# A copy moved to VectorE, fewer dummy matmuls, keys and conversion steps in another order, in the start of a delta-rule attention with a feed-forward block

## The chip, the cores and the metric

The kernel runs on one NeuronCore of a Trainium2 chip. The metric is the device time of one execution in microseconds, the median of several runs. Lower is better.

## The reference

The first half is a delta-rule recurrence over 768 positions for 4 batches of 8 heads of dimension 48. Its output, heads side by side, is the input of a feed-forward block of 384 to 2048 to 384 with the gate h * sigmoid(1.702 h).

```python
k_n = k / (np.linalg.norm(k, axis=-1, keepdims=True) + 1e-06)
for t in range(S):                       # S = 768, per batch and head, state is 48 x 48
    y[t]  = q[t] @ state
    v_old = state.T @ k_n[t]
    state = state + beta[t] * outer(k_n[t], v[t] - v_old)
x = y.transpose(0, 2, 1, 3).reshape(B * S, H * D)   # 3072 x 384
h = x @ w_in                                        # 384 x 2048
out = (h / (1 + exp(-1.702 * h))) @ w_out           # 2048 x 384
```

The two weights arrive in 64-bit floating point; the kernel fetches them raw, as pairs of 32-bit words, and makes 32-bit floats of them itself.

## The kernel before

**Tiling.** The 768 positions are cut into six chunks of 128, and a *unit* is one chunk of one batch with all eight heads: 24 units, numbered chunk by chunk (units 0 to 3 are chunk 0, units 4 to 7 chunk 1, and so on). In a unit the recurrence becomes: normalize the keys, make the Gram matrix `G` of the keys, solve a triangular system for `U` in four blocks of 32 positions, and form the outputs from `U`, the masked scores `M` and the state `ST`. Two units side by side give 256 tokens of feed-forward.

**Keys.** `normalize_mixed(n)` squares the keys of unit n on ScalarE (tile `ksq`), sums on VectorE (`ssq`), takes the root on GpSimd (`rn`), and adds, inverts and multiplies on VectorE. `prepare(n)` transposes them on PE (`psT`, copied to `kT`), makes `G` through `psG`, and for chunk 1 sends the 32-wide diagonal blocks of `G` to DRAM (`Nd`, four DMAs on the sync queue) and back in another layout into the tile `NT` (one DMA that waits for those four). The key buffers are `KN`, seven in turn; unit 7 uses `KN[0]` and unit 8 `KN[1]`.

**Inversion.** `invert(c)` inverts the 32 x 32 diagonal blocks of a whole chunk on VectorE, 128 blocks at once in the 128 partitions: 15 row steps on both 16 x 16 halves together, then a *join*: a transposed copy `X1` of the second half's inverse into a corner of `NT`, four products `P<-NT,YB` with sums into `NT`, and four products `P<-NT` with sums into `YB`. The result goes into tiles `XB`, one per unit. For chunk 0 it goes there by a transpose on VectorE, for later chunks through DRAM. Chunk 0's join copy is on ScalarE, chunk 1's on VectorE, those of later chunks on ScalarE.

**Solve.** One *hop* is a call of `together`: for some units a block solve (`psU<-V,XB`, copied to `US` or `U` on ScalarE), for others the effect of the block on the rows below (`psR<-US,G`, subtracted from `V` on VectorE). Chunk 0 is done as two pairs of units in eight hops each, with `put_out` behind each pair (`psY`, `ST`, `last`, `xT`; for the second unit of a pair six small DMAs `xT<-last` on the sync queue). Between the hops stand three kinds of other work, each handed out in fixed numbers:

- `fill(n)` advances the conversion of the weights by n steps. A piece of a weight takes five steps, on VectorE with one pass on ScalarE; the pieces of w_in are named ("in", i, e) and those of w_out ("out", f). At the end of some pieces the next raw pieces are fetched.
- `ahead_of(preparing, n)` advances the keys of chunk 1 (`keys()`) by n steps. A table of start times, `(0, 3, 6, 14, 17)`, says at which step units 4 to 8 begin.
- `warm(n)` puts n dummy matmuls on PE (`ps_warm<-ident`), which keep PE active. `NY` of them wait for a memset on VectorE and stand in chunk 0's join; `NW` stand at the start, `NU` and `NA` in the hops.

`feed()` advances the first feed-forward group of the chunk-0 tokens (`ph<-xT,w_in`, then the gate into `gT`) by half a group.

**Order.** The calls in this start are pinned (`tc.keep_in_program_order`), so each engine and each DMA queue executes them in the order in which the Python code makes them; an instruction whose operand is missing holds those behind it on its engine or queue. Behind the second pair comes a loop that converts what is left of w_in, then `invert(1)` with `feed()` in between, then the rest of `hidden`. From there on `woven(n)` runs for n = 3 to 24: it weaves the hops of neighbouring units, the keys of unit m = n + 5 and the feed-forward from `queue`. In its first steps `both_written` is in that queue, which multiplies with w_out piece by piece as the pieces are converted (`po<-w_out,gT`). The keys of units 9 and later are loaded in `follow(n)` on GpSimd's queue.

Of the kernel before, what the change touches and what calls it, by code (L numbers as in the profile page):

```python
# [18 lines left out]
def kernel(  # L19
# [32 lines left out]
    HB = 2  # L52
# [2 lines left out]
    GB = 8  # L55

    XR = DP - D
    NW, NA, NY, NU = 14, 3, 60, 11
    NQ = DFF // 4
    NPC = DFF // 8  # L60
    NS = C * C + C
# [232 lines left out]
    def fill(n):  # L294
        for _ in range(n):
            next(converting, None)
# [144 lines left out]
    def invert(c, b0=0, nb=B):  # L441

        np = nb * NB * H
        part = slice(b0 * NB * H, b0 * NB * H + np)
        N, Y = NT[part], YB[part]
        bc = bI[part, c].broadcast_to([np, BS, BS])
        tt, red = vec.tensor_tensor, vec.tensor_reduce
        if c > 0:
            tt(N, N, bc, op=ALU.mult)
            yield 0.0  # L450
        HS = BS // 2

        def dots(o, a, b, ny, nx, nk, negate):

            P = wk.tile([128, ny, nx, nk], F32, tag="P", name="P")[part]
            tt(P, a, b, op=ALU.mult)
            red(o, P, axis=AX.X, op=ALU.add, negate=negate)

        def halves(t):

            return [t[:, s * HS : (s + 1) * HS, s * HS : (s + 1) * HS] for s in range(2)]


        Yf = Y.rearrange("p j i -> p (j i)")
        Nf = N.rearrange("p i k -> p (i k)")
        step = HS * BS + HS

        def diag(t, off, dims):
            return bass.AP(t.tensor, t.offset + off, [t.ap[0], [step, 2]] + dims)

        for i in range(1, HS):
            P = wk.tile([128, 2, i, i], F32, tag="P", name="P")[part]
            tt(
                P, diag(Nf, i * BS, [[0, i], [1, i]]), diag(Yf, 0, [[BS, i], [1, i]]),
                op=ALU.mult,
            )
            red(diag(Yf, i, [[BS, i]]), P, axis=AX.X, op=ALU.add, negate=True)
            yield 0.0


        X1 = N[:, 0:HS, HS:]
        if c == 1:
            vec.tensor_copy(X1, halves(Y)[1].rearrange("p l i -> p i l"))
        else:
            act.activation(X1, halves(Y)[1].rearrange("p l i -> p i l"), ACT.Copy)
        A = N[:, 0:HS, 0:HS]
        N10, Y0 = N[:, HS:, 0:HS], halves(Y)[0]
        Q = 4
        for j in range(0, HS, Q):
            n = HS - j  # L490
            dots(
                A[:, j : j + Q, :],
                N10[:, :, j:].rearrange("p (o l) k -> p o l k", o=1).broadcast_to([np, Q, HS, n]),
                Y0[:, j : j + Q, j:].rearrange("p j (o k) -> p j o k", o=1).broadcast_to([np, Q, HS, n]),
                Q, HS, n, False,
            )
            yield 0.0
        for i in range(0, HS, Q):
            n = i + Q
            if c == 0 and i == HS - 2 * Q:  # L500
                warm(NY, vec.memset)
            dots(
                Y[:, 0:HS, HS + i : HS + i + Q],
                A[:, :, 0:n].rearrange("p j (o l) -> p j o l", o=1).broadcast_to([np, HS, Q, n]),
                X1[:, i : i + Q, 0:n].rearrange("p (o i) l -> p o i l", o=1).broadcast_to([np, HS, Q, n]),
                HS, Q, n, True,
            )
            yield 0.0
        if c == 0:
            T = wk.tile([128, BS, BS], F32, tag="P", name="YT")  # L510
            vec.transpose(T.rearrange("p d i -> p i d"), Y.rearrange("p j i -> p i j"))
            for b in range(B):
                XB = wk.tile([128, H, BS], F32, tag="XB", name="XB", bufs=4)
                tt(
                    XB, T[:, b * H : (b + 1) * H],
                    zs[:, 5, b].broadcast_to([128, H, BS]), op=ALU.mult,
                )
                inverse[b] = XB
                yield 0.0
            return  # L520
        YS = wk.tile([128, BS, BS], F32, tag="P", name="YS")[part]
        tt(YS, Y, bc, op=ALU.mult)
        dma = sync if c < 3 else nc.sync.dma_start
        groups = [range(b0, b0 + nb)]
        back = {}
        for bs in groups:
            for b in bs:
                back[b] = dram.tile([H * C, BS], F32, tag="Yd", name="Yd", bufs=4)
                dma(
                    out=back[b].rearrange("(p j) i -> p j i", j=BS),  # L530
                    in_=YS[(b - b0) * NB * H : (b - b0 + 1) * NB * H],
                )
            for b in bs:
                XB = wk.tile([128, H, BS], F32, tag="XB", name="XB", bufs=4)
                dma(out=XB, in_=back[b].rearrange("(h t) i -> t h i", h=H))
                inverse[c * B + b] = XB
        yield 0.0
# [233 lines left out]
    def run(work):  # L771
        for _ in work:
            pass
# [38 lines left out]
    def follow(n):  # L812

        dma = sync if n <= B else nc.sync.dma_start
        if n + B < len(units):
            load(n + B, ((QP, q),), dma)
        m = n - 1 + len(KN)
        if m < len(units):
            load(m, ((KN, k),), nc.gpsimd.dma_start)
        if n - 1 + B < len(units):  # L820
            load_values(n - 1 + B, dma)
        if n % HB == 0 and n > B:
            h = (n - 1) // HB
            gT = []
            queue.append(hidden(xTs[h], gT, slice(0, NTH), 1.3))
            queue.append(written(*units[h * HB], gT))
            xTs.pop(h)
# [12 lines left out]
    def woven(n, share):  # L840

        nonlocal inverting
        A, B_, D_ = steps.pop(n - 1, None), steps.get(n), steps.get(n + 1) or NoStep()
        m = n + B + 1
        K = (normalize if n > 6 else normalize_mixed)(m) if m < len(units) else iter(())
        P = prepare(m) if m < len(units) else iter(())
        if m in begun:  # L850
            K, P = iter(()), begun.pop(m)
        if n % HB == 1 and B < n and n + 1 + HB < len(units):
            inverting = invert(*units[n + 1 + HB], HB)
        ahead = STEPS[:3] if n % HB == 1 else STEPS[3:]

        next(K, None)
        together([(B_, 1)], [(A, 2)])
        run(D_.scored)
        next(K, None)
        ahead_of(inverting, ahead[0])  # L860
        spend(share / 3)

        together([(A, 3), (D_, 0)], [(B_, 1)])
        next(K, None)
        ahead_of(inverting, ahead[1])
        spend(share / 6)
        next(P, None)
        spend(share / 6)

        together([(B_, 2)], [(D_, 0)])  # L870
        if A:
            A.queries()
            A.outputs(True)
        run(P)
        ahead_of(inverting, ahead[2])
        if n % HB == 0:
            run(inverting)
        spend(share / 6)
        next(new_step(n + 2).scored, None)
        spend(share / 6)  # L880
        follow(n)
# [80 lines left out]
    def keys():  # L962

        def unit(n):
            yield from normalize_mixed(n)
            yield from prepare(n)

        begun[2 * B] = prepare(2 * B)

        def first(n):  # L970
            yield from normalize_mixed(n)
            next(begun[n])

        work = [unit(n) for n in range(B, 2 * B)] + [first(2 * B)]
        for t in range(26):
            for u, begin in enumerate((0, 3, 6, 14, 17)):
                s = t - begin
                if s >= 0 and s % 2 == 0:
                    next(work[u], None)
            yield  # L980
        for w in work:
            run(w)
# [21 lines left out]
    def feed(n=1):  # L1004
        for _ in range(n):
            while ffn and next(ffn[0], None) is None:
                ffn.pop(0)
# [8 lines left out]
    path = hops(*pair[2:])  # L1016
    for i in range(2 * NB):
        together(*next(path))
        fill(2)
        if i > 2:  # L1020
            feed()
        warm(NU if i < 3 else 4)
        ahead_of(preparing, 2)
        if 3 <= i < 6:
            fetch_out(i - 3)
    for s in pair[2:]:
        put_out(s)
        feed()
        fill(2)
    ffn.append(hidden(xTs[1], gTs[1], slice(0, NTH), 1.3, True))  # L1030
    xTs.pop(0), xTs.pop(1)
    load(B + 2, ((QP, q),), sync)
    while not ("in", 3, 1) in done:
        fill(2)
        feed()
        ahead_of(preparing, 1)
    run(preparing)
    first = new_step(B)
    run(first.scored)
    inverting = invert(1)  # L1040
    for i in range(25):
# [41 lines left out]
```

## Time and profile before

| | |
|---|---|
| median of the runs | 792.83 us (3 runs, 791.43 to 795.32) |
| the profiled execution | 792.6 us, span of its profile 790.9 us |
| mean granted TensorE clock | 0.965 |
| PE busy | 754.1 us (95% of the span) |
| PE weight load busy | 564.5 us (71%) |
| VectorE (DVE) busy | 456.5 us (58%) |
| ScalarE (ACT) busy | 243.0 us (31%) |
| GpSimd (POOL) busy | 127.1 us (16%) |
| dummy matmuls `ps_warm` | 199, 29.9 us |

Times are microseconds from the start of the span. PE is the matmul side of TensorE, PEld its weight load, SPq the sync engine's DMA queue. A line of a timeline gives start, length, engine, source line, operation, output<-input, sizes and count, and in brackets how long the engine was idle ahead of it and what ended that. A line of the waits gives who waited for whom, the time in total, the number of times and the longest. The slices are 40 equal parts of the span, 19.8 us each, with the busy share in tenths. A list of instructions shows a float matmul twice, since it is made in two passes. Nearly all source lines are the helper's line 102, so rows are told apart by their tiles.

### The profile page before, as it was taken

How to read it: one execution, taken by the hardware profiler on the slowest of the kernel's cores; microseconds unless marked ns; L12 is line 12 of the kernel's file. 1: busy time of each engine (PE TensorE's matmuls, PEld its weight loads, DVE VectorE, ACT ScalarE, POOL GpSimd, SP SyncE). 2: the span in 40 equal slices, each digit the busy share in tenths (PEclk: the TensorE clock that was granted, in tenths of full speed). 3: DMA queues.
4: the chain of work that ended last, by engine and by line, in shares of the span. 5: the costliest groups of instructions: out<-in, count | busy, mean ns of one | idle time of the engine just before them, and what ended most of it. 6: DMA issues, size and time to landing. Idle time of an engine off the chain costs nothing.

```text
span 790.9 us, 18899 instructions
## 1 busy us (share of the span) xinstructions
PE 754.1 (95%) x8199; PEld 564.5 (71%) x8199; DVE 456.5 (58%) x934; ACT 243.0 (31%) x537; POOL 127.1 (16%) x132
## 2 busy tenths in 40 slices
PE   7788999598899999999999999999999999999997
PEld 6677888355568768768678678678678678677684
DVE  6778778996895666766666766756756531100000
ACT  4555552244233323223223223223223123121110
POOL 6301410001121212212212211221210000000000
PEclk8589999799999999999999999999999999999999
DMA  9941940453323231231222232241230020000000
GB/s 164 176 58 39 256 96 8 111 162 72 75 64 70 55 86 42 58 90 35 64 74 52 56 95 43 46 103 42 46 76 12 21 43 2 12 15 1 25 1 20
DMA packets 130657, 50.72 MB, mean 64 GB/s; under 512 B 105408, under 2 KB 126016, under 8 KB 130576
## 3 DMA queue, kind: packets, MB, share of 16 engines
q1 hardware_dynamic: 128112, 41.08, 24.1%
q0 software_dynamic: 2464, 8.46, 4.4%
q8 instruction: 64, 1.05, 0.6%
q14 instruction: 17, 0.14, 0.1%
HBM read 32.08 MB, written 16.25 MB: 61 GB/s over the span
## 4 chain that ended last, share of the span: by engine, by line
PE 81%; DVE 12%; DMA 3%; ACT 2%; issue 2%; SPq 1%; POOL 0%; DVEq 0%; POOLq 0%; ACTq 0%
PE po L102 28%; PE ph L102 26%; PE psY L102 5%; PE psU L102 5%; PE psQ L102 4%; PE psG L102 4%; PE ps_warm L102 3%; PE psT L102 3%; DVE P L102 3%; DVE YB L102 2%; DVE w_out L102 2%; PE psR L102 2%; DVE tmp L102 2%; DMA Nd<-G 1%; DVE NT L102 1%
## 5 line engine op out<-in xcount | busy, mean ns | idle before, releaser
L102 PE MATMUL po<-w_out,gT 128*128 128x384 f32 x768 | 269.5, 500 | 11.7 <-ACT w_out L102 8.9
L102 PE MATMUL ph<-xT,w_in 128*128 128x256 f32 x1152 | 261.5, 383 | 0.3
L102 PEld LDWEIGHTS ph<-xT,w_in 128*128 128x128 f32 x1152 | 214.7, 190 | 32.7 <-issue 1.5
L102 PEld LDWEIGHTS po<-w_out,gT 128*128 128x128 f32 x768 | 143.1, 193 | 103.9 <-ACT w_out L102 9.3
L102 DVE TENSOR_TENSOR V<-V,psR 64x384 f32<-64x384 f32 (+1 forms) x96 | 53.4, 556 | 198.0 <-PE psR L102 192.7
L102 ACT ACTIVATE gT<-ph 128x512 f32<-128x512 f32 x96 | 56.5, 596 | 140.1 <-PE ph L102 140.0
L102 DVE TENSOR_TENSOR P<-NT,YB 64x8 f32<-64x8 f32 (+31 forms) x190 | 89.2, 469 | 5.3
L102 ACT COPY US<-psU 32x384 f32<-32x384 f32 x92 | 43.2, 469 | 146.1 <-PE psR L102 128.6
L102 DVE TENSOR_REDUCE YB<-P 64x4 f32<-64x8 f32 (+31 forms) x190 | 80.9, 426 | 6.5
L102 PEld LDWEIGHTS psU<-V,XB 32*32 32x32 f32 x1536 | 57.9, 106 | 35.4 <-issue 29.0
L102 PE MATMUL psU<-V,XB 32*32 32x48 f32 x1536 | 68.6, 204 | 1.5 <-DVE YB L102 1.2
L605 POOL TENSOR_SCALAR_AFFINE_SELECT M<-M 128x1024 f32<-128x1024 f32 x20 | 24.9, 1247 | 265.9 <-DVE M L102 169.4
L102 PE MATMUL psR<-US,G 32*32 32x48 f32 x2208 | 60.4, 204 | 0.0
L102 PEld LDWEIGHTS psR<-US,G 32*32 32x32 f32 x2208 | 51.1, 106 | 1.1 <-ACT G L102 0.5
L102 PE MATMUL psQ<-QS,kT 48*128 48x176 f32 (+1 forms) x384 | 37.6, 341 | 3.7 <-ACT QS L102 3.7
L102 DVE TENSOR_TENSOR P<-NT 64x256 f32<-64x256 f32 (+7 forms) x40 | 34.0, 851 | 4.8 <-ACT NT L102 4.6
L102 PEld LDWEIGHTS psQ<-QS,kT 48*128 48x128 f32 x384 | 31.1, 209 | 6.8 <-ACT QS L102 5.6
L102 PE MATMUL ps_warm<-ident 128*128 128x256 bf16 x199 | 29.9, 309 | 5.4 <-DVE ps_warm L102 4.0
L102 PE MATMUL psG<-kT 48*128 48x128 f32 x384 | 32.3, 306 | 2.6 <-ACT kT L102 1.3
L102 DVE TENSOR_REDUCE NT<-P 64x64 f32<-64x1024 f32 (+7 forms) x40 | 32.6, 815 | 1.4
L87 POOL DMA_DIRECT2D KN<-in_k_dram x15 | 14.3, 951 | 111.5 <-PE psY L102 102.6
L102 PEld LDWEIGHTS psG<-kT 48*128 48x128 f32 x384 | 27.3, 205 | 6.0 <-ACT G L102 2.1
(98 smaller groups left out, 604.2 us busy)
## 6 DMA issues: line engine op xcount, KB each, us to landing
Nd<-G SPq DMA_DIRECT2D x16, 512.0 KB, 3.5
QP<-in_q_dram SPq DMA_DIRECT2D x24, 192.0 KB, 3.8
V<-in_v_dram SPq DMA_DIRECT2D x24, 192.0 KB, 3.3
out_dram<-o SPq DMA_DIRECT2D x24, 192.0 KB, 1.9
KN<-in_k_dram POOLq DMA_DIRECT2D x15, 192.0 KB, 3.7
NT<-Nd SPq DMA_DIRECT2D x20, 128.0 KB, 2.5
Yd<-YS SPq DMA_DIRECT2D x20, 128.0 KB, 2.4
XB<-Yd SPq DMA_DIRECT2D x20, 128.0 KB, 3.3
```

The source lines that it names most:

```text
L87: dma(out=dst[n % len(dst)][:, :, 0:D], in_=src[b, :, c * C : (c + 1) * C, :].rearrange("h p d -> p h d"),)
L102: return lambda *a, **kw: tc.keep_in_program_order(op(*a, **kw))
L605: (pool if self.n < B else nc.gpsimd).affine_select(out=self.M, in_=self.M, compare_op=ALU.is_gt, fill=0.0, base=0, pattern=[[0, H], [1, 1 ...
```

## The change

It changes the order and the number of instructions in the first 200 us; the arithmetic is the same.

- Chunk 0's join copy goes from ScalarE to VectorE (`c <= 1`).
- `NY` is 46 in place of 60, and the memset that releases these dummies stands behind the first of the join's second four products instead of the second.
- In the second pair's hops the dummies are put only in the first three hops; the four dummies in each of the other five are gone.
- The second pair's hops advance the conversion by 3 steps in place of 2 from the sixth hop on, and so does each of its two `put_out`.
- Units 7 and 8 begin their keys at steps 10 and 13 in place of 14 and 17.
- The keys of units 9 and 10 are loaded on the sync queue behind the second pair, and not on GpSimd's; they are normalized one `woven` step sooner (in n = 3 and n = 4).
- Unit 4's first step (its scores) is begun ahead of the loop that converts the rest of w_in and finished in its second turn, and not behind it.

```diff
@@ -55,7 +55,7 @@
     GB = 8
 
     XR = DP - D
-    NW, NA, NY, NU = 14, 3, 60, 11
+    NW, NA, NY, NU = 14, 3, 46, 11
     NQ = DFF // 4
     NPC = DFF // 8
     NS = C * C + C
@@ -479,7 +479,7 @@
 
 
         X1 = N[:, 0:HS, HS:]
-        if c == 1:
+        if c <= 1:
             vec.tensor_copy(X1, halves(Y)[1].rearrange("p l i -> p i l"))
         else:
             act.activation(X1, halves(Y)[1].rearrange("p l i -> p i l"), ACT.Copy)
@@ -497,7 +497,7 @@
             yield 0.0
         for i in range(0, HS, Q):
             n = i + Q
-            if c == 0 and i == HS - 2 * Q:
+            if c == 0 and i == HS - 3 * Q:
                 warm(NY, vec.memset)
             dots(
                 Y[:, 0:HS, HS + i : HS + i + Q],
@@ -815,7 +815,7 @@
         if n + B < len(units):
             load(n + B, ((QP, q),), dma)
         m = n - 1 + len(KN)
-        if m < len(units):
+        if 2 * B + HB < m < len(units):
             load(m, ((KN, k),), nc.gpsimd.dma_start)
         if n - 1 + B < len(units):
             load_values(n - 1 + B, dma)
@@ -845,10 +845,13 @@
         nonlocal inverting
         A, B_, D_ = steps.pop(n - 1, None), steps.get(n), steps.get(n + 1) or NoStep()
         m = n + B + 1
-        K = (normalize if n > 6 else normalize_mixed)(m) if m < len(units) else iter(())
+        if n < B + HB:
+            K = normalize_mixed(m + 1) if n <= B else iter(())
+        else:
+            K = (normalize if n > 6 else normalize_mixed)(m) if m < len(units) else iter(())
         P = prepare(m) if m < len(units) else iter(())
         if m in begun:
-            K, P = iter(()), begun.pop(m)
+            P = begun.pop(m)
         if n % HB == 1 and B < n and n + 1 + HB < len(units):
             inverting = invert(*units[n + 1 + HB], HB)
         ahead = STEPS[:3] if n % HB == 1 else STEPS[3:]
@@ -972,8 +975,8 @@
             next(begun[n])
 
         work = [unit(n) for n in range(B, 2 * B)] + [first(2 * B)]
-        for t in range(26):
-            for u, begin in enumerate((0, 3, 6, 14, 17)):
+        for t in range(22):
+            for u, begin in enumerate((0, 3, 6, 10, 13)):
                 s = t - begin
                 if s >= 0 and s % 2 == 0:
                     next(work[u], None)
@@ -1016,26 +1019,34 @@
     path = hops(*pair[2:])
     for i in range(2 * NB):
         together(*next(path))
-        fill(2)
+        fill(2 if i < 5 else 3)
         if i > 2:
             feed()
-        warm(NU if i < 3 else 4)
+        else:
+            warm(NU)
         ahead_of(preparing, 2)
         if 3 <= i < 6:
             fetch_out(i - 3)
     for s in pair[2:]:
         put_out(s)
         feed()
-        fill(2)
+        fill(3)
     ffn.append(hidden(xTs[1], gTs[1], slice(0, NTH), 1.3, True))
     xTs.pop(0), xTs.pop(1)
     load(B + 2, ((QP, q),), sync)
+    for n in range(2 * B + 1, 2 * B + 1 + HB):
+        load(n, ((KN, k),), sync)
+    first = new_step(B)
+    next(first.scored)
+    t = 0
     while not ("in", 3, 1) in done:
         fill(2)
         feed()
+        if t == 1:
+            run(first.scored)
         ahead_of(preparing, 1)
+        t += 1
     run(preparing)
-    first = new_step(B)
     run(first.scored)
     inverting = invert(1)
     for i in range(25):
```

## The prediction

> **What bounds the kernel now.** I read the page's slices first, then the waits, the timeline engine by engine, and the chain of waits.
>
> ```profile
> PE   7788999598899999999999999999999999999997
> DVE  6778778996895666766666766756756531100000
> PEclk8589999799999999999999999999999999999999
> ```
>
> A slice is 19.8 us. From slice 9 on PE is full, so the end moves only by what the first 200 us release: PE idle, dummies, or a late start of whatever holds PE there. From 121 to 187 us the timeline of VectorE has no pause over 0.1 us: it inverts chunk 1 (121.43 to 148.1) and converts w_out to 187.1. PE ran out of `ph` at 143.0 and waited for the first converted piece of w_out. So the start of that inversion, at 121.43, sets the end. The waits up to 200 us:
>
> ```profile
> PE po L102 <- ACT w_out L102: 8.9, 1, 8.9
> DVE P L102 <- ACT NT L102: 4.6, 1, 4.6
> PE psT L102 <- DVE KN L102: 2.3, 1, 2.3
> ```
>
> First: that gap of PE. Second: VectorE waits for chunk 0's join copy, which stands on ScalarE behind the scores' copies. Third: unit 9's transpose waits for its normalized keys; unit 10's waits 2.38 us more at 204.31. Timelines (start, length) of the first join:
>
> ```profile
> 38.35 0.66 ACT L102 ACTIVATE NT<-YB 128x256 f32<-128x256 f32 x1
> 39.04 0.86 DVE L102 TENSOR_TENSOR P<-NT 128x256 f32<-128x256 f32 x1 [4.55 <-ACT NT L102]
> 41.80 9.33 PE L102 MATMUL ps_warm<-ident 128*128 128x256 bf16 x60 [4.01 <-DVE ps_warm L102]
> ```
>
> The sync queue's, which explains 121.43 (the inversion's multiply shows "3.05 <-issue"):
>
> ```profile
> 82.35 1.01 SPq L102 DMA_DIRECT2D KN<-in_k_dram  x2
> 94.77 3.28 SPq L102 DMA_DIRECT2D Nd<-G  x4
> ...
> 109.50 0.31 SPq L102 DMA_DIRECT2D NT<-Nd  x1
> 109.86 3.68 SPq L102 DMA_DIRECT2D xT<-last  x6
> 113.58 0.58 SPq L102 DMA_DIRECT2D QP<-in_q_dram  x1
> 114.27 2.00 SPq L102 DMA_DIRECT2D Nd<-G  x4
> 119.26 0.32 SPq L102 DMA_DIRECT2D NT<-Nd  x1
> ```
>
> Unit 7's pair `Nd`, `NT` comes last, behind six `xT` pieces. And ScalarE in the second pair's third hop and later:
>
> ```profile
> 79.30 0.47 ACT L102 COPY US<-psU 32x384 f32<-32x384 f32 x1 [0.77 <-PE psR L102]
> 82.73 1.08 ACT L102 ACTIVATE G<-psG 128x512 f32<-128x512 f32 x2 [2.96 <-PE psG L102]
> 83.84 0.47 ACT L102 COPY U<-psU 32x384 f32<-32x384 f32 x1
> ...
> 90.70 0.53 ACT L102 ACTIVATE ksq<-KN 128x384 f32<-128x384 f32 x1
> ```
>
> **What the Trainium skill says.** "TensorE: Matmul & The Clock Gate", Part 1: PE starts at half clock, about 3.4 us of activity release it, an idle window takes it back. The trace agrees: granted clock 0.50 from 40.4 to 47.2, 1.00 from 47.2 to 51.0, and 0.60 from 77.2 to 81.5 after PE pauses of 1.35 and 0.68 us. The same page, "Architectural detail": ScalarE and VectorE are strict FIFO; the join copy at 38.35, right behind the `M` copies, agrees. "SBUF — State Buffer", "SBUF: two separate sides": VectorE with two SBUF inputs and GpSimd block each other; the same 256-element product took 0.86 us beside a GpSimd select at 38.53 and 0.42 at 33.62. "DMA: Bandwidth & Descriptors", "Anatomy of one DMA": a DMA's wait is made on the issuing sequencer, so it holds what is queued behind; each `NT` above issues 3 us after its `Nd` and holds the rest.
>
> **The change part by part**, against the profiled execution: 792.6 us, span 790.9 and 1.7 around it; the median of the runs is 792.83.
>
> 1. *Join copy on VectorE.* It goes behind the last row step (end 27.52). It costs 0.4 (chunk 1's took 0.39 at 133.61); the four products to 34.49 then end at 34.9. The second half took 39.04 to 46.0; one more GpSimd select now lies over it (+0.44): end 42.3. Transpose 1.96, first `XB` 0.36: inverse of unit 0 at 44.7, before at 48.4. ScalarE loses 0.55 us ahead of the scaling of V (7.3 us, end 45.7, needed for the first hop's copy only).
> 2. *46 dummies for 60, one product earlier.* PE is free at 37.8. At 0.213 us cold and 0.109 warm (from 60 in 9.33 us with the clock rising at 47.2), 46 end between 44.1 (clock up at 40.4) and 45.8 (at 43.8). So the first solve starts at 44.8 to 45.9 instead of 51.05: **gain s = 5.6** (5.15 to 6.25). The first pair's hops (2.11 us each, PE full, VectorE half idle) and its outputs keep their order and move by s.
> 3. *Keys of units 7 and 8 four steps sooner.* Unit 7's square now stands on ScalarE right behind the `US` copy (79.30), ahead of the `G` and `U` copies, and needs the key load issued at 82.35, behind six `xT` and twelve w_in pieces. Moved by s: issue 76.75; landing took 5.5 us, other loads of keys 3.7 to 7.0; I take 5.0, since GpSimd's load of w_out now comes after it: 81.75. ScalarE is free at 74.2, so it **waits about 7.5 us**. Behind it are two `G` copies (1.09), `U` (0.47) and, through `U`, the next hop's psR, VectorE's V and all that follows: `U` ends at 81.75+0.53+1.09+0.47 = 83.85, against 84.3-5.6 = 78.7 without the wait: 5.1 lost on the hops. PE then pauses some 4 us; one window at half clock costs 0 to 1.7, I take 1.2.
> 4. *No dummies from the fourth hop, three steps a fill from the sixth.* 20 dummies of 0.11 are 2.2 us less of PE, but unit 7's and 8's transposes and unit 7's Gram product (0.44+0.44+1.09) come into the hops from behind. Hops five to eight on PE: 3.4, 2.7, 3.8, 2.3 us, outputs with one `ph` group 4.45. End: 83.85+16.65+1.2 = 101.7 (before 102.8). Five conversion steps (0.7 each) move in beside this; VectorE needs 13.9 us from 82.7, ready at 96.6, so they cost nothing here; without that cover they would cost 3.5.
> 5. *VectorE behind the pair.* Sum of its rows after the second ST: 11.2 us (twelve conversion steps, four V of unit 4). Inversion ready at 101.9+11.2 = **113.1**. Unit 4's scores come sooner; PE delivers psQ from 106.8, VectorE reaches V at 107.5: nothing.
> 6. *Sync queue.* Unit 7's `Nd`, `NT` now precede `xT` and QP. First `Nd` 94.77-5.6 = 89.2; four pairs as before without 4.3 us: last `NT` lands at 121.43-5.6-4.3 = 111.5, with the measured 3.4 us of the third pair 110.3. Gram products are there in time. So VectorE is last, not the queue, and the inversion starts at 113.1: **gain 8.3**. `xT` of the second pair lands near 115; its first `ph` is due at 117.
> 7. *Keys of units 9 and 10.* Loads go from GpSimd's queue to the sync queue behind QP: two issues of 0.4 near 114, with the queue idle from 119.6 to 148.1 before; due after 135. Unit 9's 1.48 us (0.55+0.16+0.20+0.57) now fall among the w_out steps, VectorE full: -1.48; one step went ahead of the inversion: +0.36. Unit 9's psT no longer waits, but w_out's piece at 185.2 holds PE instead: 0. Unit 10's stall, where PE is full, goes: +2.38. Next there are unit 11's keys; VectorE has 0.32, 0.89 and 0.76 us of waits for PE before them and 0.93 less work, so it keeps up.
>
> Sum: 8.3+0.36-1.48+2.38 = 9.6 us; 792.6-9.6 = **783.0**.
>
> **Rivals.**
> A. *The keys land early enough or the stall is covered.* For: its load's wait on its eighth predecessor may be shorter with GpSimd's loads later. Against: seventeen sync issues, 11 us, stand before it. Then the queue bounds: start 110.3, gain 11.1+1.26 = 12.4: 780.2. Chance 0.20.
> B. *The loads of w_out and raw, pushed later by the wait, run into the Nd/NT pairs.* 2.3 MB at the 327 GB/s seen from 88 to 95 us is 7 us; if pairs take 7 instead of 5, the last `NT` is at 118 and the gain 3.4+1.26 = 4.7, or with half of s lost about 2: 788 to 791. Against: DMA was as full before. Chance 0.17.
> C. *Slower: ScalarE's wait for unit 7's keys.* Each us of later landing moves the hops and the inversion by one. From 81.75, the gain of 9.6 is used up at 91.4, that is 14.6 us after issue. For: V loads in the same stretch took 10.2; against: keys took 5.5 there. At 96 it gives 797. Chance 0.08.
> Mine: 0.55.
>
> **Numbers.** The range takes s (1.1), landing (3.7 to 7), clock (1.7), A whole and most of B: 778 to 788.5. Half a percent, 4 us, is about what a measurement of this kernel can tell from no change: limits 788.9 and 796.8. Faster 0.81 (mine, A, a third of B), same 0.14 (the rest of B, a part of C), slower 0.05.
>
> **What would show it.** Right: no wait of VectorE at the first join; first psU at 45 to 46; ScalarE idle before unit 7's square on the key load by 6 to 9 us with PE idle behind it; `NT<-NT,bI` at 113 directly behind a conversion step; no psT wait of unit 10. Wrong: no such wait on ScalarE (A); the multiply waiting for `NT` beyond 116 (B); the square after 90 (C); or PE waiting longer for w_out after 150 than 1.5 us a time.

## Result and the profile after

The changed kernel takes 783.05 us (median of 4 runs, 782.55 to 783.69), the kernel before beside it 792.55 us: ratio 0.9875, interval 0.9849 to 0.9902. In a later comparison it took 782.26 us against 789.63: 0.9897 (0.9870 to 0.9924). The kernel before spreads more (787 to 795 us), and with more runs its median was 789.6 to 789.9 in three comparisons; so the gain is rather 7 us (7.4 in the later comparison) than the 9.5 of the first four runs. The predicted 783.0 holds, and so does the predicted gain of 9.6 beside those first runs; beside the later ones it is 2 us too large. Some of its terms do not hold, and that their errors cancel is luck; this is the main matter of what follows. Three of the single runs behind the medians below took over 1.5% longer than the fastest of their kernel; the ratios leave them out, the medians do not.

The profiled execution took 782.8 us, span 780.8. Its page, the slices of 19.5 us:

```profile
PE   7898799699999999999999999999999999999997
DVE  5989679987977566666666666666665531000000
PEclk8599899879999999999999999999999999999999
```

Behind the slice with PE's gap (the 6) every slice of PE but the last shows 9. Before, two slices behind the gap showed 8, those with the key stalls of units 9 and 10. VectorE's last digits end one slice sooner. The waits up to 200 us (who waited for whom, total, times, longest):

```profile
ACT ksq L102 <- DMA KN<-in_k_dram: 7.2, 1, 7.2
PE po L102 <- ACT ksq L102: 5.2, 1, 5.2
PE psT L102 <- ACT G L102: 4.6, 3, 3.3
```

VectorE's wait for the join copy and PE's waits for normalized keys are gone. ScalarE's wait for a key load is new, and PE waits behind it. PE's gap before w_out shrank from 8.9 to 5.2 us. The timeline of the first join (start, length):

```profile
27.67 0.77 DVE L102 COPY NT<-YB 128x256 f32<-128x256 f32 x1
...
42.17 1.99 DVE L102 STREAM_TRANSPOSE YT<-YB 128x1024 f32<-128x1024 f32 x1
...
37.71 6.67 PE L102 MATMUL ps_warm<-ident 128*128 128x256 bf16 x46
44.73 0.83 PE L102 MATMUL psU<-V,XB 32*32 32x48 f32 x16 [0.35 <-issue]
```

The first solve starts at 44.73 instead of 51.05, 6.32 us sooner. Before, the dummies held it: they ended at 51.13, while the inverse of unit 0 was there at 48.4. Now the dummies end at 44.38 and the inverse comes at 44.6. Then the sync queue, ScalarE and PE in the second pair's third hop:

```profile
75.00 1.80 SPq L102 DMA_DIRECT2D KN<-in_k_dram  x2
...
80.70 0.52 ACT L102 ACTIVATE ksq<-KN 128x384 f32<-128x384 f32 x1 [7.24 <-DMA KN<-in_k_dram]
81.25 1.09 ACT L102 ACTIVATE G<-psG 128x512 f32<-128x512 f32 x2
82.36 0.47 ACT L102 COPY U<-psU 32x384 f32<-32x384 f32 x1
...
81.90 1.12 PE L102 MATMUL psT<-ident,KN 128*128 128x128 f32 x4 [3.28 <-ACT G L102]
```

The `G` and `U` copies stand behind the waiting square, as the prediction had it. The end of the second pair, the start of chunk 1's inversion (its first multiply, `NT<-NT,bI`) and the sync queue:

```profile
103.23 0.36 DVE L102 TENSOR_TENSOR ST<-psY,ST 128x192 f32<-128x192 f32 x1 [0.95 <-PE psY L102]
...
114.68 0.35 DVE L102 TENSOR_SCALAR tmp<-raw 128x384 int32<-128x384 int32 x1
114.95 1.22 DVE L102 TENSOR_TENSOR NT<-NT,bI 128x1024 f32<-128x1024 f32 x1
...
107.06 0.31 SPq L102 DMA_DIRECT2D NT<-Nd  x1
107.42 3.69 SPq L102 DMA_DIRECT2D xT<-last  x6
```

No bracket behind 114.95: the inversion comes straight behind a conversion step, 11.72 us after the last `ST`. The last `NT` was issued at 107.06, ahead of the `xT` pieces, so the queue no longer holds it. And the transposes of units 9 and 10 on PE:

```profile
178.13 0.60 PE L102 MATMUL psT<-ident,KN 128*128 128x128 f32 x4
...
196.42 0.60 PE L102 MATMUL psT<-ident,KN 128*128 128x128 f32 x4
```

Neither waits; before, each waited 2.35 to 2.38 us.

Where the 10.1 us between the two spans (790.9 and 780.8) came from, cut at the start of the inversion and at its last product, `YS<-YB,bI`, before and after:

```profile
146.85 1.23 DVE L102 TENSOR_TENSOR YS<-YB,bI 128x1024 f32<-128x1024 f32 x1
...
141.11 1.22 DVE L102 TENSOR_TENSOR YS<-YB,bI 128x1024 f32<-128x1024 f32 x1
```

Start 121.43 to 114.95, 6.48 gained; the inversion itself 25.42 to 26.16, 0.74 lost; from `YS` to the end 644.05 to 639.7, 4.35 gained. The prediction had 8.3, nothing, and 0.36 - 1.48 + 2.38 = 1.26.

### The profile page after: what moved, and what is told of

Read it like the earlier page. It is cut to its first block, busy times and chain, and to the rows that moved or that the text cites. A ratio compares the mean times of both kernels' runs of the same rounds, so it can differ in the third digit from the quotient of the medians.

```text
span 780.8 us, 18832 instructions
## 1 busy us (share of the span) xinstructions
PE 753.3 (96%) x8165; PEld 564.1 (72%) x8165; DVE 457.1 (59%) x935; ACT 243.1 (31%) x536; POOL 125.3 (16%) x130
## 4 chain that ended last, share of the span: by engine, by line
PE 83%; DVE 11%; DMA 3%; ACT 2%; issue 1%; SPq 0%; POOL 0%; DVEq 0%; POOLq 0%; ACTq 0%
PE po L102 29%; PE ph L102 27%; PE psU L102 5%; PE psY L102 5%; PE psQ L102 4%; PE psG L102 4%; PE psT L102 3%; DVE P L102 3%; PE ps_warm L102 2%; PE psR L102 2%; DVE YB L102 2%; DVE tmp L102 2%; DVE w_out L102 1%; DVE NT L102 1%; DMA KN<-in_k_dram 1%
## 5 line engine op out<-in xcount | busy, mean ns | idle before, releaser
L102 ACT ACTIVATE gT<-ph 128x512 f32<-128x512 f32 x96 | 56.5, 596 | 140.1 <-PE ph L102 140.0
L102 ACT COPY o<-po 128x384 f32<-128x384 f32 x24 | 11.5, 479 | 61.7 <-issue 39.2
L102 ACT COPY M<-psQ 128x256 f32<-128x256 f32 x68 | 22.9, 377 | 22.2 <-DVE V L102 16.1
```

What stands on the lines that cost most here:

```text
L102: return lambda *a, **kw: tc.keep_in_program_order(op(*a, **kw))
```

## The experiments

The kernels of one comparison ran on one chip beside the kernel before. Executions of one kernel spread over 1 to 13 us. The changed kernel's two medians, 783.05 and 782.26, agree, and 782.7 is the base to which the other medians are held; single effects are read from the profiles. In every diff of this section "+" is what the experiment has.

### Four parts taken back, one at a time

Base: the changed kernel, which itself did not run in this comparison. The kernel before took 789.64 us in it (787.42 to 794.02).

**Keys of units 9 and 10 as before.**

```diff
-        if 2 * B + HB < m < len(units):
+        if m < len(units):
             load(m, ((KN, k),), nc.gpsimd.dma_start)
...
-        if n < B + HB:
-            K = normalize_mixed(m + 1) if n <= B else iter(())
-        else:
-            K = (normalize if n > 6 else normalize_mixed)(m) if m < len(units) else iter(())
+        K = (normalize if n > 6 else normalize_mixed)(m) if m < len(units) else iter(())
...
-            P = begun.pop(m)
+            K, P = iter(()), begun.pop(m)
...
-    for n in range(2 * B + 1, 2 * B + 1 + HB):
-        load(n, ((KN, k),), sync)
```

> The changed kernel with the keys of units 9 and 10 as before (loads on GpSimd's queue, normalized in n = 4 and n = 5); all else changed. Theory (the trace after): the two stalls of PE on these keys cost 2.35 and 2.38 us and a stretch at half clock behind each (about 1.6 us each), so their removal is worth 5 to 7 us net of 1.48 us of VectorE moved and of new waits of 1.24 and 0.64; this kernel then takes 788 to 790 us, inversion of chunk 1 at 115 as in the changed kernel. Rival (step 7 of the prediction, only unit 10's stall counts, net 0.9): 784.

Measured: 785.8 us, ratio 0.9941 (0.9915 to 0.9967), span 782.7. The two waits are back:

```profile
176.06 0.76 PE L102 MATMUL psT<-ident,KN 128*128 128x128 f32 x4 [2.35 <-DVE KN L102]
...
197.23 1.09 PE L102 MATMUL psT<-ident,KN 128*128 128x128 f32 x4 [2.38 <-DVE KN L102]
```

`YS` stands at 140.16, so 642.5 us remain to the end, against 639.7. That is 2.8 us by the profile, and 3.1 by the medians (785.8 and 782.7): more than the prediction's 1.26, less than the theory named here.

**Keys of units 7 and 8 late.**

```diff
-        for t in range(22):
-            for u, begin in enumerate((0, 3, 6, 10, 13)):
+        for t in range(26):
+            for u, begin in enumerate((0, 3, 6, 14, 17)):
```

> The changed kernel with units 7 and 8 beginning their keys at steps 14 and 17 again. Theory (keys sooner bought the queue's order and paid for it with ScalarE's 7.2 us wait, so the two cancel): no wait of ScalarE on a key load, hops end some 5 us sooner, but unit 7's Nd and NT again stand behind xT, QP and now also two key loads on the sync queue, so the inversion starts at 121.4 - 6.3 + 1.4 = 116.5, bound by NT, against 114.95; time 783 to 785. Rival 1 (the wait is cheap, the queue's order is the gain): inversion at 116.5 but VectorE no sooner, 787. Rival 2 (the wait is all that counts): 778 to 779.

Measured: 783.4 us, ratio 0.9902 (0.9875 to 0.9928). ScalarE and VectorE:

```profile
83.01 0.52 ACT L102 ACTIVATE ksq<-KN 128x384 f32<-128x384 f32 x1 [0.18 <-DMA KN<-in_k_dram]
...
116.58 1.23 DVE L102 TENSOR_TENSOR NT<-NT,bI 128x1024 f32<-128x1024 f32 x1 [9.71 <-issue]
```

The long wait of ScalarE is gone and VectorE is ready at 106.9, but now it idles 9.71 us: unit 7's `NT` was issued at 114.42. Starting the keys sooner buys the queue's order and pays with ScalarE's wait; the two cancel, as the theory said.

**The first join as before.**

```diff
-    NW, NA, NY, NU = 14, 3, 46, 11
+    NW, NA, NY, NU = 14, 3, 60, 11
...
-        if c <= 1:
+        if c == 1:
...
-            if c == 0 and i == HS - 3 * Q:
+            if c == 0 and i == HS - 2 * Q:
```

> The changed kernel with chunk 0's join copy on ScalarE, 60 dummies behind the second product. Theory (the first join shifts all that follows up to the inversion): first psU at 51.05 instead of 44.73, everything behind 6.3 us later, inversion at 121.3; of that VectorE's and PE's stretch behind passes on all: 789 to 790. Rival (a later stage absorbs a part, since PE was not bound by VectorE alone from 150 on): 785 to 787.

Measured: 787.14 us, ratio 0.9957 (0.9942 to 0.9972). The first solve is at 49.51, 4.78 later than in the profile of the changed kernel, and the inversion at 119.50, 4.55 later. The span is 783.9, 3.1 longer. So two thirds of what reached the inversion reached the end in this execution, and the rest was absorbed before the last converted piece of w_out, which came 2.9 later. That is the rival's side. The median is 4.4 above the base, which is nearer to all of it; the two are not told apart.

**The hops' steps and dummies as before.**

```diff
-        fill(2 if i < 5 else 3)
+        fill(2)
...
-        else:
-            warm(NU)
+        warm(NU if i < 3 else 4)
...
-        fill(3)
+        fill(2)
```

> The changed kernel with the second pair as before: fill(2) throughout, four dummies in each of the last five hops, keys still sooner. Theory (hops end PE-bound and VectorE's tail is on the path): hops 2.2 us later by the dummies, less what they keep of the clock (0 to 2), and five conversion steps, 3.5 us, moved behind the hops; inversion 3.5 to 5.5 us later at 118.5 to 120.5; time 786 to 788.5. Rival (NT on the queue is as late as VectorE, and PE has slack behind): under 1 us, 783 to 784.

Measured: 786.97 us, ratio 0.9965 (0.9948 to 0.9982). From the last `ST` (107.80) to the inversion (123.27) 15.47 us pass, against 11.72: the five conversion steps, 3.75 us, are in VectorE's tail again. The first pair was over 3 us slower as well, with a clock of 0.84 from 50 to 60 us, so the span of 788.3 overstates the edit. The median, 4.3 above the base, lies where the theory put it. The inversion took 25.39 us here, as before the change (25.42), against 26.16 in the changed kernel: the 0.74 us lost in it belongs to these edits; why is open. What the missing dummies alone are worth was not tried.

### Join alone, the key wait taken away, a gap filled

**The changed kernel again,** with no edit.

> The changed kernel once more, beside the kernel before on this chip and beside the three kernels that run with it, for the sizes of the single edits. Expected: the ratio of the first runs, 0.9875 within 0.003.

Measured: 782.26 us, ratio 0.9897 (0.9870 to 0.9924), span 778.9. The same program on the same data, but with the inversion three microseconds sooner:

```profile
100.15 0.36 DVE L102 TENSOR_TENSOR ST<-psY,ST 128x192 f32<-128x192 f32 x1 [0.95 <-PE psY L102]
111.87 1.22 DVE L102 TENSOR_TENSOR NT<-NT,bI 128x1024 f32<-128x1024 f32 x1
```

**Keys of units 7 and 8 loaded on GpSimd's queue,** issued behind the first pair's outputs.

```diff
     for s in pair[:2]:
         put_out(s)
         fill(2)
-    load(7, ((KN, k),), sync)
-    load(8, ((KN, k),), sync)
+        load(s.n + 7, ((KN, k),), other_queue)
```

> The changed kernel with the key loads of units 7 and 8 on GpSimd's queue, each right behind the outputs of a unit of the first pair, instead of on the sync queue behind them. Theory (ScalarE's wait of 7.2 us for unit 7's keys costs the second pair's hops about 5 us, and behind them VectorE is last, not the sync queue): the keys come in time, ScalarE's wait is under 1.5 us, the second ST stands at 97 to 99 instead of 103.2, the inversion of chunk 1 starts at 109 to 111 (then bound by the last NT); two thirds of this pass on to the end: 2.5 to 4 us faster than the changed kernel. Rival (the wait only fills time that the half clock or the loads would take anyway): the inversion at 113 or later and under 1 us of gain. Second rival (the keys' bytes now delay V and the w_out pieces of the same queue): a new wait of ScalarE or GpSimd between 75 and 95 and no gain.

Measured: 776.72 us, ratio 0.9824 (0.9793 to 0.9855), against 0.9897 of the changed kernel beside it: 5.5 us faster, and faster than both kernels. GpSimd's issue, ScalarE's square, VectorE:

```profile
63.50 1.86 POOL L102 DMA_DIRECT2D KN<-in_k_dram  x2
...
73.68 0.53 ACT L102 ACTIVATE ksq<-KN 128x384 f32<-128x384 f32 x1
...
97.75 0.36 DVE L102 TENSOR_TENSOR ST<-psY,ST 128x192 f32<-128x192 f32 x1 [0.94 <-PE psY L102]
109.46 1.22 DVE L102 TENSOR_TENSOR NT<-NT,bI 128x1024 f32<-128x1024 f32 x1
```

The load is issued at 63.50 instead of 75.00 and the square does not wait. The pair ends at 97.75 and the inversion starts at 109.46, where the theory had both. It was wrong in two things: the last `NT` was issued at 104.66, and VectorE, not the queue, is still last; and the gain of 5.5 us is more than the 2.5 to 4 it expected. No new wait for a load appears on GpSimd or ScalarE. With the two key loads off the sync queue the loads behind them, `QP` and `V`, also go out 2.5 and 3.3 us sooner; what that is worth was not tried apart.

**The join alone,** on the kernel before.

```diff
-    NW, NA, NY, NU = 14, 3, 60, 11
+    NW, NA, NY, NU = 14, 3, 46, 11
...
-        if c == 1:
+        if c <= 1:
...
-            if c == 0 and i == HS - 2 * Q:
+            if c == 0 and i == HS - 3 * Q:
```

> The kernel before with the first join's edits alone: its copy on VectorE, one product earlier, 46 dummies for 60. Theory (the join moves the first pair by 6.3 us, the last NT behind the six xT pieces then bounds the inversion, and the key waits of units 9 and 10 with their half clock stay): first psU at 45, the inversion at 115.5 to 117 with VectorE waiting for NT, psT waits of 2.3 us twice; 4 to 6 us faster than before, ratio 0.9925 to 0.995. Rival (the join carries the whole gain, the rest of the change cancels): ratio 0.988 or less. Second rival (the 6 us are absorbed by the w_out stretch): ratio over 0.997.

Measured: 783.09 us, ratio 0.9907 (0.9878 to 0.9937). VectorE and PE:

```profile
114.58 1.23 DVE L102 TENSOR_TENSOR NT<-NT,bI 128x1024 f32<-128x1024 f32 x1 [3.66 <-issue]
...
177.16 0.63 PE L102 MATMUL psT<-ident,KN 128*128 128x128 f32 x4 [2.36 <-DVE KN L102]
...
199.48 0.63 PE L102 MATMUL psT<-ident,KN 128*128 128x128 f32 x4 [1.98 <-DVE KN L102]
```

The mechanism is the theory's: the inversion waits for `NT`, and both key stalls stay. The size is 6.5 us, between the theory and the first rival. Beside the whole change (782.26) it is 0.8 us apart, with overlapping intervals: in the medians the join alone carries nearly all of the gain. Yet the rest without the join was worth 2.5 us above (787.14 against 789.64), so the parts do not add up: 6.5 and 2.5 for a whole of 7.4. The copy, the number of dummies and their place were changed together only.

**Dummies in PE's gap before w_out,** on the changed kernel.

```diff
     while ffn:
         feed()
+    warm(44)
     queue = [both_written(0, gTs[0]), written(*units[HB], gTs[1])]
```

> The changed kernel with 44 dummy matmuls (about 4.8 us) in the gap of PE at 139 to 144 us, where it has run out of ph and waits for the first converted piece of w_out. Theory A (the loss of some 2.5 us between the inversion's end and the last piece of w_out is due to the half clock behind that gap, 0.66 and 0.65 in the stretches from 140 and 160): clock 1.00 from 140 to 170, the po matmuls from 144 take half as long, VectorE's wait of 1.4 us for psR near 163 goes, the last piece of w_out comes 1 to 2.5 us earlier, the total falls by 1 to 2.5 us. Theory B (VectorE is full there and PE only waits for it): PE waits longer for w_out between 150 and 165, the last piece of w_out within 0.5 us of the changed kernel, no difference in the total.

Measured: 783.55 us, ratio 0.9923 (0.9895 to 0.9952): no gain in the total. By the profile the clock was 1.00 from 100 to 160, and 40.6 us passed from `YS` (145.67) to the start of VectorE's last step on w_out (186.26), against 42.2 after (141.11 to 183.31). But the version with keys on GpSimd's queue took 40.6 there too, without these dummies. So a half clock may cost 1.6 us in that stretch, but the dummies are no reliable cure. What this execution showed besides is more telling. Up to 139 us its instructions are those of the changed kernel, and yet the second `ST` and the inversion stand here:

```profile
107.79 0.36 DVE L102 TENSOR_TENSOR ST<-psY,ST 128x192 f32<-128x192 f32 x1 [0.95 <-PE psY L102]
119.50 1.22 DVE L102 TENSOR_TENSOR NT<-NT,bI 128x1024 f32<-128x1024 f32 x1
```

The same program has now started this inversion at 111.87, 114.95 and 119.50. Stretches of this execution (busy time by engine, then PEclk, DMA share and GB/s):

```profile
86.00:90.00 4.00, 4.00 (x51) 3.19 (x49) 1.00 (x2) 1.69 (x3) 2.77 (x3) 0.50 0.98 360
90.00:94.00 4.00, 4.00 (x20) 3.02 (x22) 3.03 (x7) 1.48 (x3) 0.00 (x0) 0.50 0.80 276
94.00:98.00 4.00, 4.00 (x36) 2.87 (x32) 2.75 (x6) 0.79 (x2) 0.00 (x0) 0.50 0.39 78
```

Behind ScalarE's wait PE runs at half clock for 17.1 us (82.10 to 99.20), though it shows as busy. The first profile of the changed kernel had two half-clock stretches, 71.45 to 74.90 and 81.70 to 88.55; the second only one, 71.35 to 81.65.

### Keys of units 9 and 10 alone, dummies in the hops, the kernel before again

**Earlier keys of units 9 and 10 alone,** on the kernel before.

```diff
-        if m < len(units):
+        if 2 * B + HB < m < len(units):
             load(m, ((KN, k),), nc.gpsimd.dma_start)
...
+        if n < B + HB:
+            K = normalize_mixed(m + 1) if n <= B else iter(())
...
+    for n in range(2 * B + 1, 2 * B + 1 + HB):
+        load(n, ((KN, k),), sync)
     while not ("in", 3, 1) in done:
```

> The kernel before with the earlier keys of units 9 and 10 alone (loads on the sync queue behind the second pair, normalized one unit ahead). Theory (the stalls for these keys and the half clock behind them are worth 3 to 3.5 us from the inversion's end to the kernel's end, whatever else is done): no psT wait over 0.5 us of units 9 and 10, span minus start of the inversion's last product (YS) at 638 to 641 us instead of 644, less about 1 us because the two key issues now stand ahead of the last Nd and NT: 2 to 3 us faster than before, ratio 0.996 to 0.998. Rival (the record's sum, 0.9 us): span minus YS at 643, ratio 0.999 or more.

Measured: 789.39 us against 789.94, ratio 0.9988 (0.9969 to 1.0007): not told apart from no change. The sync queue and the inversion:

```profile
114.08 1.29 SPq L102 DMA_DIRECT2D KN<-in_k_dram  x2
115.47 2.43 SPq L102 DMA_DIRECT2D Nd<-G  x4
120.73 0.32 SPq L102 DMA_DIRECT2D NT<-Nd  x1
...
122.90 1.23 DVE L102 TENSOR_TENSOR NT<-NT,bI 128x1024 f32<-128x1024 f32 x1 [4.00 <-issue]
```

In the old order the two key issues stand ahead of the last `Nd` and `NT`, and the inversion starts 1.5 us later. From `YS` (148.31) to the end it took 640.3, as the theory had it. So the profile backs the theory and the median the rival. A part of what the same edit gains behind the inversion, 1.5 us, is lost at the queue, where the queue is the bound; that leaves over 2 us by the profiles, and why the median does not show them is open.

**24 dummies for 11 in the second pair's first hop,** on the version with keys on GpSimd's queue.

```diff
-            warm(NU)
+            warm(NU if i else 24)
         ahead_of(preparing, 2)
```

> The version with unit 7's and 8's key loads on GpSimd's queue, with 24 dummies instead of 11 in the second pair's first hop, where PE waited 1.35 us for a kT copy before its clock fell to 0.50 for about 5 us. Theory (that pause brings the half clock): clock 1.00 from 70 to 78, the second ST 1 to 2.5 us sooner than 97.75, the inversion at 107 to 108.5; up to 1.5 us faster than that version's ratio of 0.9824. Rival (the second pause of 0.68 us, or something else, brings the half clock): clock still 0.5 there and no gain, or 0.1 us of loss.

Measured: 776.45 us (median of five runs, one of which took 785.58; 775.2 without it), ratio 0.9819 (0.9794 to 0.9845), not told apart from the version without (776.72, 0.9824). The stretch from 70 us and the inversion:

```profile
70.00:80.00 10.00, 9.32 (x222) 7.88 (x222) 9.30 (x16) 6.43 (x13) 1.86 (x2) 1.00 0.75 183
...
107.71 1.22 DVE L102 TENSOR_TENSOR NT<-NT,bI 128x1024 f32<-128x1024 f32 x1
```

In the profiled execution (span 772.3) the half clock is gone from this stretch and the inversion is 1.75 us sooner, both as expected. Whether that reaches the median, five runs do not show.

**The same with 44 more in the gap before w_out** (the two edits together).

> The same as with 24 dummies, and 44 more in PE's gap before the first converted piece of w_out. Theory: with both pauses filled no half clock is left from 70 to 170, the times of single runs lie closer together, and the median is the lowest of all: ratio 0.978 to 0.982. Rival (VectorE alone sets the stretch from 110 to 180, which took 40.59 us with and without a slow clock): as with 24 dummies alone, within 0.5 us.

Measured: 776.47 us, ratio 0.9840 (0.9818 to 0.9863). In its profile the clock was 1.00 from 60 to 150, but 0.83 from 40 to 60 and 0.62 from 150 to 160, where nothing had been filled. The theory's lowest median and its ratio of 0.982 or less did not come; the rival is nearer, and these dummies show no gain.

**The kernel before, a second profile.**

> The kernel before once more, for a second profile. The first was of an execution of 792.6 us. Theory (how far PE's half clock behind the pauses at 74 to 77 us reaches differs from execution to execution): the first pair the same to 0.1 us, the inversion's start between 117 and 123, and the span different by as much as the inversion. Rival (the order is fixed): the inversion at 121.4 within 0.5 us.

Measured: 794.85 us (one run), span 793.1.

```profile
105.56 0.36 DVE L102 TENSOR_TENSOR ST<-psY,ST 128x192 f32<-128x192 f32 x1 [1.68 <-PE psY L102]
121.31 1.23 DVE L102 TENSOR_TENSOR NT<-NT,bI 128x1024 f32<-128x1024 f32 x1 [0.18 <-issue]
```

The hops ended 2.75 us later than in the first profile (102.81), with a clock of 0.62 from 80 to 90, and the inversion came at the same time (121.31 and 121.43): VectorE's idle time ahead of it shrank from 3.05 to 0.18. So in these two executions the hops vary, as the theory said, and the start of the inversion does not, as the rival said: the queue hid the hops' variation there. The span is 2.2 us longer all the same, 0.75 of it in the inversion and 1.6 behind `YS`. In the changed kernel VectorE follows the hops directly, and their variation moves the inversion.

## Why the prediction was right

**Steps 1 and 2, the join: right.** First solve at 44.73 for 44.8 to 45.9; s was 6.3 for 5.6. The copy took 0.77 for 0.4, since it began inside a GpSimd select (27.11 to 28.20); this is the slowdown that the prediction had read from the 0.86 us product. In the seven executions in which the copy began inside that select it took 0.50 to 0.77 us and ended 0.23 to 0.25 after the select; in the three in which it began ahead of it, it took 0.39 to 0.40. It cost nothing visible, as the whole chain still came out sooner.

**Step 3, the key wait: right in mechanism and size.** 7.24 us for 7.5; `U` ended at 82.83 for 83.85. That it costs the hops is shown by loading the keys sooner: from the first solve to the last `ST` that version took 53.8 us, the changed kernel 55.4, 58.5 and 63.3 in three executions, so the wait, with the half clock about it, cost 1.6 to 9.6 us, and the predicted 5.1 and 1.2 lie inside; the medians lie 5.5 us apart. For the hops as a whole the prediction had 56.5 (45.4 to 101.9). In its profile `U` came 1.0 sooner than predicted and the last `ST` 1.3 later, so the stretch between took 2.3 us more than the sum had. The half clock is the likely term: one window of it was allowed, at 0 to 1.7 us with 1.2 taken, and there it lasted 6.85 us, two of them.

**Step 4, the moved steps: right.** Back in the tail, they cost 3.75 for the 3.5 named as the price without cover. (Its end, 101.7, is used as 101.9 in step 5.)

**Step 5, VectorE's tail: right.** 11.72 for 11.2.

**Step 6, the queue: right.** VectorE is last; the last `NT` was issued at 107.06. But 113.1 as the start of the inversion was one value for something that lies between 111.87 and 119.50. The gain there was 6.5 in the profiled execution, not 8.3.

**Step 7, the keys of units 9 and 10: the step that was mis-sized.** It gave them 0.9 us (2.38 less 1.48). Over all profiles, from `YS` to the end:

| keys of units 9 and 10 | executions | us from `YS` to the end |
|---|---|---|
| as before | 4 (before twice, join alone, keys 9 and 10 taken back) | 642.5, 643.3, 644.05, 645.6: mean 643.9 |
| sooner | 10 (all others) | 638.2 to 641.0: mean 639.7 |

The two sets do not overlap, and their means lie 4.2 us apart. Two things were left out. Unit 9's stall, 2.35 us, was put at nothing, because a piece of w_out would hold PE there instead; with the keys in time no such wait came (178.13 above). That is most of the 3.1 us missing. And each stall was priced at its length alone, while the matmuls behind it ran slow: in the kernel before, unit 10's transpose took 1.09 us for 0.60, and the clock was 0.83 from 200 to 210. How the rest divides was not measured. The slices that the prediction opens with held a sign of it: it calls PE full from slice 9 on, but slices 9 and 10, with these two stalls, show 8. In medians the worth is smaller: 3.1 us when it is taken back, and 0.55 when done alone, where 1.5 was lost at the queue. Why the medians show less than the profiles is open. Both profiles of the kernel before were of executions above its median of 789.6 (792.6 and 794.9), so its usual execution may not have the whole of these costs; none of those was profiled. The granted clocks of the runs point to the half clock: of the 52 executions of the kernel before in the first comparison of experiments, the nine slowest (792.7 to 794.0 us) had 0.959 to 0.961, the nine fastest (787.4 to 788.7) 0.966 to 0.972.

So the total was right because an overestimate of 1.8 us at the inversion (8.3 for 6.48) and 0.74 us in it stood against an underestimate of 3.1 behind it (1.26 for 4.35). The direction and the mechanisms of steps 1 to 6 were foreseen; that these errors left only 0.5 us was luck. The base helped as well: the sum starts from an execution of 792.6 us, while the later medians of the kernel before lie 3 us lower.

**The rivals.** A, the key wait not there, was not what happened; made to happen by an earlier load it gave 776.7, a gain of 12.9 us on the 789.63 beside it, for A's 12.4. The inversion then starts at 109.46, close to A's 110.3, but on VectorE and not on the queue, which A had as the bound. B did not occur: the four `NT` went out 3.5 to 5.8 us apart and VectorE came after them. C, slower through a late landing, did not occur: the square could start 5.7 us after the key load's issue (75.00 to 80.70).

**The sign.** 0.81 for faster was well placed: the edits of the join alone secure it (ratio 0.9907), and it needs none of the rest.

## What to carry to other kernels

Taking a long wait off the chain moves everything behind it, but then ask which load's issue has not moved with it: here a key load stood too far back on a DMA queue, and issuing it 11.5 us sooner on another queue brought 5.5 us more, beside 7.4 for the whole change in that comparison. Where a queue was the bound, it also hid the variation of the engines ahead of it; once it is gone, that variation moves the start of what follows (111.87 to 119.50 us here), so give such a start as a range. How much of it reaches the end is not shown: the ten runs of the changed kernel lie within 2.8 us (780.9 to 783.7), those of the kernel before within 8.5. Do not put a PE stall at nothing, in a stretch where PE is full, because something else may hold PE there; look for that wait in the trace, and allow for slow matmuls behind the stall.

## What the runs showed of the hardware that was not expected

The half clock behind a PE pause is not a fixed price. Read in steps of 0.05 us, it comes in whole pieces of about 3.43 us, and what differs is how many:

| execution | half clock, us from the start | length | pieces |
|---|---|---|---|
| changed kernel, first profile | 71.45 to 74.90 | 3.45 | 1 |
| | 81.70 to 88.55 | 6.85 | 2 |
| changed kernel, second profile | 71.35 to 81.65 | 10.30 | 3 |
| keys of units 9 and 10 as before | 70.60 to 77.45 | 6.85 | 2 |
| | 84.25 to 87.70 | 3.45 | 1 |
| dummies in the gap before w_out | 82.10 to 99.20 | 17.10 | 5 |

All four programs are the same up to 99 us. Behind the same two pauses of PE, 1.35 and 0.68 us long (the second near 70 us), came one piece, three, two and none; behind the pause that ended at 81 or 82 us came two, one and five (the second profile had no such pause, as PE was still at half clock when the wait ended). The Trainium skill, "TensorE: Matmul & The Clock Gate", Part 1, says that the window which watches PE runs free of the program and lasts about 3.4 us, which fits these pieces and a start that differs between executions. It also says that one window of sustained work releases the clock and that one idle window takes it back. Neither fits all of these traces: the two pauses are both shorter than a piece, where the prediction had read its trace as agreeing, and PE showed as busy for 12 us on end at 0.50 in the stretches from 86 to 98 us above. The hops there are many small matmuls (32x48); whether these count as too little work was not tried.
